# Loading tile 0's x in two halves on two queues, and the parameter transposes one warm-up later

## Chip, cores and metric

The kernel runs on one core of one Trainium2 chip. The metric is the device time of one execution in microseconds (us). The time before is the median of three runs.

## The reference

Two blocks share one layer norm and are added to the residual. Cut to what matters:

```
xn = layernorm(x)                                   # x: 1 x 2048 x 512
A  = 2*Re(sum over states of C * h) + xn*Dskip      # h[t] = Lam_bar*h[t-1] + B_bar*xn[t]
B  = (silu(xn @ w_gate) * (xn @ w_up)) @ w_down     # 512 -> 1376 -> 512
out = x + A + B
```

The state recurrence runs over the 2048 rows with 512 complex states. `Lam_bar` and `B_bar` come from the parameter vectors `log_dt`, `Lambda_re` and `Lambda_im`, of 512 numbers each. Inputs and output are bfloat16.

## The kernel before

The 2048 rows are 16 tiles of 128 rows, in four chunks of four tiles (512 rows). A chunk goes through layer norm, a transposition of the normalised rows (`xnT`), gate and up products, the products with B for the state recurrence, the scan on VectorE, and one accumulated product that joins `w_down` and C. TensorE's instructions and SyncE's are issued in the order in which the program states them (`_CHAIN`). The order on ScalarE, VectorE and GpSimd is chosen by `_schedule`, a list planner with estimated costs: among what could start soonest, within 200 ns, it takes the work with the longest remaining path (plus priorities written by hand). It models the transfers as one pipe that takes them one after the other. `_plan` then gives each DMA a semaphore of its own with a level of 16, and each engine one counting semaphore, and derives the waits.

What the change touches is the start, before TensorE has anything real to do:

- Loads. SP issues, in this order, x of tiles 0, 1 and 2 (128 rows of 1 KB each, `ldx`, all through L438), three slices of `w_gate` by rows of the contraction, x of tile 3, the fourth slice, then larger loads. ACT's queue issues the three parameter loads (`pload`, 4 rows of 256 bytes into `prow`); ScalarE's first activation, with its table load, stands behind the first of them in the trace.
- Statistics of tiles 0, 1 and 3 on VectorE (`ln_stats`: L533 `bn_stats`, L535 `bn_aggr`), then the power -1/2 on GpSimd (L537), and scaling on VectorE (L544) in two parts, columns 0 to 127 and 128 to 511 for tiles 0 and 1. Tile 2's statistics are taken on ScalarE (L552, L554) with GpSimd's L556 and L558, and it is scaled by L567.
- Transposes on TensorE (`xt_part`, L642) of each part, and their evacuation to `xnT`, on VectorE for the first part (L649) and on ScalarE for the others (L654).
- Gate products of the first six column tiles of `w_gate` in quarters (`ffn_gate_quarters`, L835): one matmul of 128 columns for each column tile, row tile and slice of the contraction, ordered by hand so that each uses what has come in by then. From L807 on, products use whole chunks of 512 columns.
- Ahead of all this TensorE runs warm-up matmuls on a constant (`pe_warm`, L508): n of 512 columns and m of 128. Between them stand three small transposes of the parameters (`params_t`, L517), which need the three parameter loads.

TensorE's order at the start is written out thus:

```
pe_warm(7, 0, ta)
params_t(tc)
pe_warm(1, 3, ta)
xt_part(c, 0, 0, ta)
ev00 = xt_part_ev_dve(c, 0, 0, ta)
xt_part(c, 0, 1, tc)
```

Of the kernel before, what the change touches and what calls it, by code (L numbers as in the profile page):

```python
# [31 lines left out]

class _Task:
    __slots__ = ("eng", "fn", "deps", "name", "est", "idx", "dma", "sem", "lvl",
                 "waits", "nsig", "vc", "out", "lat", "bl", "start", "fin", "nbytes", "prio", "ninst", "odeps")

    def __repr__(self):
        return "T(%s,%s)" % (self.eng, self.name)
# [2 lines left out]
class _Graph:  # L41
# [5 lines left out]
    def add(self, eng, fn, reads=(), writes=(), name="", est=100.0, dma=False, after=(), out=False, nbytes=0, prio=0.0, ninst=1, order=()):  # L47
        t = _Task()
        t.eng, t.fn, t.name, t.est, t.dma, t.out, t.nbytes, t.prio = eng, fn, name, float(est), dma, out, nbytes, prio
        t.ninst = ninst  # L50
        t.idx = len(self.tasks)
        deps = set(after)
        for r in reads:
            w = self.last_w.get(r)
            if w is not None:
                deps.add(w)
        for r in writes:
            w = self.last_w.get(r)
            if w is not None:
                deps.add(w)  # L60
            for rd in self.readers.get(r, ()):
                deps.add(rd)
        for r in reads:
            self.readers[r].append(t)
        for r in writes:
            self.last_w[r] = t
            self.readers[r] = []
        deps.discard(t)
        t.deps = deps
        t.odeps = set(o for o in order if o is not None and o not in deps)  # L70
        assert all(o.eng == eng for o in t.odeps)
        t.sem = None
        t.lvl = 0
        t.lat = 0.0
        self.tasks.append(t)
        return t

# [111 lines left out]
def _plan(tasks, streams, new_sem, eng_sems):  # L189
    consumers = defaultdict(list)  # L190
    for t in tasks:
        for d in t.deps:
            consumers[d].append(t)
    for t in tasks:
        if t.dma:
            t.nsig = True
        else:
            t.nsig = any((c.eng != t.eng) or (t.eng != "pe") or c.dma for c in consumers[t])
    last_out = [None, 0]
    for eng, st in streams.items():  # L200
        lvl = 0
        for t in st:
            if t.dma and t.out and not consumers[t]:
                if last_out[0] is None:
                    last_out[0] = new_sem("out_end")
                t.sem = last_out[0]
                last_out[1] += 16
                t.lvl = last_out[1]
            elif t.dma:
                t.sem = new_sem("dma%d" % t.idx)  # L210
                t.lvl = 16
            elif t.nsig:
                lvl += 1
                t.sem = eng_sems[eng]
                t.lvl = lvl
    end_wait = tuple(last_out)
    pos = {e: 0 for e in streams}
    known = {e: {} for e in streams}
    done = set()
    remaining = sum(len(s) for s in streams.values())  # L220
    while remaining:
        progressed = False
        for eng, st in streams.items():
            while pos[eng] < len(st):
                t = st[pos[eng]]
                if any(d not in done for d in t.deps):
                    break
                kn = known[eng]
                waits = {}
                for d in t.deps:  # L230
                    if d.eng == eng and eng == "pe" and not d.dma and not t.dma:
                        continue
                    k = id(d.sem)
                    if kn.get(k, 0) >= d.lvl:
                        continue
                    if k not in waits or waits[k][1] < d.lvl:
                        waits[k] = (d.sem, d.lvl)
                for d in t.deps:
                    for k, v in d.vc.items():
                        if kn.get(k, 0) < v:  # L240
                            kn[k] = v
                t.waits = list(waits.values())
                t.vc = dict(kn)
                if t.sem is not None:
                    t.vc[id(t.sem)] = max(t.vc.get(id(t.sem), 0), t.lvl)
                done.add(t)
                pos[eng] += 1
                remaining -= 1
                progressed = True
        assert progressed, "deadlock in static schedule"  # L250
    outs = [t for t in tasks if t.out]
    held = set()
    todo = [t for t in outs if not consumers[t]]
    while todo:
        t = todo.pop()
        if t not in held:
            held.add(t)
            todo.extend(t.deps)
    assert all(t in held for t in outs)
    return end_wait  # L260
# [11 lines left out]
def bass_parallel_sum__ssm_conv_s5__swiglu_ffn__prompt_kernel(  # L272
# [32 lines left out]
    with es:  # L305
        block = es.enter_context(nc.Block())

        def sb(name, shape, dt):
            return es.enter_context(nc.sbuf_tensor(name, shape, dt))
# [7 lines left out]
        x_sb = sb("x_sb", [128, NT, D], B16)  # L317
# [35 lines left out]
        st = sb("st", [128, NT, 9], F32)  # L353
# [9 lines left out]
        def one_c(n):  # L363
            return nc.const_aps.tensor(1.0, [128, n], B16)
# [57 lines left out]
        def BK(b):  # L422
            return [("bk", b, 0), ("bk", b, 1)]

        x_v = A_x[0].rearrange("(a p) d -> p a d", p=128)
# [5 lines left out]
        def dma(name, dst, src, writes, nbytes, reads=(), after=(), out_=False, eng="sp", xpose=False, prio=0.0, **kw):  # L431
            after = tuple(after)
            if xpose:
                assert eng == "sp"
                fn = lambda e, dst=dst, src=src: e.dma_start_transpose(out=dst, in_=src)
                est, nb = 2000.0, int(nbytes * 1.45)
            else:
                fn = lambda e, dst=dst, src=src: e.dma_start(dst, src, **kw)  # L438
                est, nb = 330.0 + nbytes / 900.0, nbytes
            t = g.add(eng, fn, reads=reads, writes=writes, name=name, dma=True, after=after, out=out_, est=est, nbytes=nb, prio=prio)  # L440
            return t

        TILEB = 128 * D * 2
        FH0 = 6 * 128

        def pload(name, slot, src, **kw):
            dma(name, prow[:, slot, :], src.rearrange("(a p) -> a p", p=128), [("prow", slot)], 1024, **kw)
# [3 lines left out]

        def ldx(a):
            return dma("ld_x%d" % a, x_sb[:, a:a + 1, :], x_v[:, a:a + 1, :], [("x", a)], TILEB)
        pload("ld_ldt", 2, A_log_dt, eng="act")
        pload("ld_lim", 1, A_Lambda_im, eng="act")
        pload("ld_lre", 0, A_Lambda_re, eng="act")
        ldx(0)
        ldx(1)
        ldx(2)
        ldw(0)  # L460
        ldw(1)
# [22 lines left out]
        def loads_wd():  # L484
# [9 lines left out]
              reads=[("ones",)], writes=[("ident",)], name="ident", est=300)  # L494
        g.add("pool", lambda e: e.iota(iot[:], pattern=[[1, TP]], base=0, channel_multiplier=0, allow_small_or_imprecise_dtypes=True),
              writes=[("iot",)], name="iota", est=1000)
# [5 lines left out]
              name="act_warm", est=220, prio=1e6)  # L502

        def pe_warm(n, m, bk):

            def mm(e):
                for w in [512] * n + [128] * m:
                    inst = e.matmul(pbank[:, bk, 0:w], lhsT=one_c(128), rhs=one_c(w), start=True, stop=True)  # L508
                return inst
            g.add("pe", mm, writes=BK(bk), name="pe_warm", est=n * 427 + m * 107, ninst=n + m)  # L510
# [20 lines left out]

        def ln_stats(a, order=()):
            ln_bn[a] = g.add("dve", lambda e, a=a: e.bn_stats(out=st[:, a, 0:6], in_=x_sb[:, a, :]),  # L533
                             reads=[("x", a)], writes=[("st", a)], name="bnst%d" % a, est=640, order=order)
            ln_ag[a] = g.add("dve", lambda e, a=a: e.bn_aggr(out=mv[:, a, :], in_=st[:, a, :]),  # L535
                             reads=[("st", a), ("steps",)], writes=[("mv", a)], name="bnag%d" % a, est=90)
            ln_rs[a] = g.add("pool", lambda e, a=a: e.tensor_tensor(out=rstd[:, a:a + 1], in0=mv[:, a, 1:2], in1=mhalf[:, a:a + 1], op=ALU.pow),  # L537
                  reads=[("mv", a), ("mhalf",)], writes=[("rstd", a)], name="rstd%d" % a, est=600, prio=(3000.0 if a < 4 else 0.0))
# [284 lines left out]
        def ffn_gate_quarters(c, tiles):  # L823
            ta, tb = next_tr(), next_tr()
# [23 lines left out]
                    xt_part_ev(c, a, h, slot)  # L848

            tc = banks[tiles[-1]]  # L850
            pe_warm(7, 0, ta)
            params_t(tc)
            pe_warm(1, 3, ta)
            xt_part(c, 0, 0, ta)
            ev00 = xt_part_ev_dve(c, 0, 0, ta)
            xt_part(c, 0, 1, tc)
# [27 lines left out]
            for i in tiles:  # L884
# [6 lines left out]
                      reads=BK(bk), writes=[("sg", sl)], name="silu%d_%d" % (c, i), est=490)  # L891
# [293 lines left out]
```

## Time and profile before

| what | value |
|---|---|
| median of 3 runs | 178.64 us (178.61 to 178.97) |
| profiled execution | 178.72 us |
| its span, first to last instruction | 177.0 us |
| TensorE matmul busy | 173.4 us (98%) |
| VectorE busy | 162.0 us (92%) |
| ScalarE busy | 101.4 us (57%) |
| GpSimd busy | 15.1 us (9%) |
| moved by DMA | 12.91 MB |

Times in the profile count from the start of the span. A line of the timeline gives start, duration, engine, source line, operation, output and inputs, and in brackets how long the engine was idle before and what ended that. "SPq" and "ACTq" are the issues of transfers on the queues of SyncE and ScalarE; "PEld" is the weight load of TensorE, which overlaps its matmuls. The recorded time of one matmul includes its way through the array; what one costs in a dense row is the distance between starts.

### The profile page before, as it was taken

The page shows a single profiled execution, that of the slowest core. Times are in us where ns is not written, and L with a number is a line of the kernel's source. Part 1 is how long each engine was busy: PE and PEld are TensorE (multiplying, and loading weights), DVE is VectorE, ACT ScalarE, POOL GpSimd, SP SyncE. Part 2 cuts the span into 40 slices and gives each one's busy share as a digit, 9 for nine tenths or more (in the row PEclk, how much of TensorE's full clock was granted, in tenths as well). Part 3 has the DMA queues.
Part 4 walks back from the last instruction along what each step waited for, and adds up shares of the span by engine and source line. Part 5 has one row for each costly group of instructions (what it writes and reads, how often), then busy time and mean ns, then how long its engine had stood idle before and what let it go on. Part 6 is the DMA issues. An engine that isn't in the chain of part 4 may idle for free.

```text
span 177.0 us, 2634 instructions
## 1 busy us (share of the span) xinstructions
PE 173.4 (98%) x948; PEld 86.5 (49%) x956; DVE 162.0 (92%) x342; ACT 101.4 (57%) x201; POOL 15.1 (9%) x38
## 2 busy tenths in 40 slices
PE   8999999999999999999999999999999999999994
PEld 2884644455444444446444444445544444444743
DVE  3687899999989979999999999999999999999983
ACT  4679999999998739896598500620666610000000
POOL 6630500000000280000000000000000000000000
DMA  5999669793000700002008000001110000001012
GB/s 149 267 362 250 118 122 171 181 343 131 0 4 0 148 0 0 0 16 77 32 0 150 0 4 0 0 0 59 59 33 0 2 0 0 0 4 59 30 59 89
DMA packets 25092, 12.91 MB, mean 73 GB/s; under 512 B 17304, under 2 KB 25080, under 8 KB 25080
## 3 DMA queue, kind: packets, MB, share of 16 engines
q1 hardware_dynamic: 25056, 12.75, 28.4%
q8 instruction: 7, 0.11, 0.3%
q14 instruction: 5, 0.04, 0.1%
q10 hardware_dynamic: 24, 0.00, 0.0%
HBM read 6.46 MB, written 2.10 MB: 48 GB/s over the span
## 4 chain that ended last, share of the span: by engine, by line
PE 98%; issue 0%; DVE 0%
PE pb L807 36%; PE pb L1041 21%; PE pb L952 16%; PE pb L1054 16%; PE pb L835 3%; PE pb L917 3%; PE pb L508 2%; PE pb L642 1%; DVE osb L1066 0%; PE pb L517 0%
## 5 line engine op out<-in xcount | busy, mean ns | idle before, releaser
L807 PE MATMUL pb<-xnT,wgu 128*128 128x512 bf16 x296 | 64.7, 379 | 0.0
L807 PEld LDWEIGHTS pb<-xnT,wgu 128*128 128x128 bf16 x296 | 28.9, 98 | 33.7
L994 DVE TENSOR_TENSOR_SCAN vq<-sm,car,vq 128x512 bf16<-128x512 f32 x32 | 39.7, 1274 | 0.1
L1041 PE MATMUL pb<-wd,hT 128*128 128x512 bf16 (+3 forms) x194 | 38.1, 355 | 0.2
L1041 PEld LDWEIGHTS pb<-wd,hT 128*128 128x128 bf16 (+1 forms) x198 | 18.5, 98 | 19.9
L952 PE MATMUL pb<-xnT,BT 128*128 128x512 bf16 x128 | 28.1, 379 | 0.0
L1054 PE MATMUL pb<-W,hss 128*128 128x512 bf16 (+2 forms) x140 | 27.8, 355 | 0.2
L956 ACT ACTIVATE u_sb<-pb 128x512 bf16<-128x512 f32 x32 | 18.6, 594 | 13.2 <-PE pb L952 12.4
L902 ACT ACTIVATE uf<-pb 128x512 bf16<-128x512 f32 x40 | 23.5, 606 | 4.3 <-PE pb L807 2.7
L820 ACT ACTIVATE sg<-pb 128x512 bf16<-128x512 f32 x34 | 20.4, 600 | 2.8 <-PE pb L807 2.6
L1054 PEld LDWEIGHTS pb<-W,hss 128*128 128x128 bf16 x144 | 13.5, 98 | 14.2
L952 PEld LDWEIGHTS pb<-xnT,BT 128*128 128x128 bf16 x128 | 12.5, 98 | 15.1
L904 DVE TENSOR_TENSOR hT<-sg,uf 128x512 bf16<-128x512 bf16 x40 | 16.5, 418 | 2.1 <-ACT uf L902 1.3
L1066 DVE TENSOR_TENSOR osb<-pb,x_sb 128x512 bf16<-128x512 f32 (+2 forms) x18 | 11.2, 627 | 1.7 <-PE pb L1054 1.2
L985 DVE TENSOR_TENSOR scrA<-u_sb,cosT 128x1024 bf16<-128x1024 bf16 x16 | 11.0, 687 | 0.6 <-ACT cosT L772 0.5
L988 DVE TENSOR_TENSOR scrA<-u_sb,sin 128x1024 bf16<-128x1024 bf16 x16 | 11.0, 687 | 0.0
L1004 DVE TENSOR_TENSOR scrA<-vq,sin 128x1024 bf16<-128x1024 bf16 x16 | 11.0, 687 | 0.0
L1000 DVE TENSOR_TENSOR scrA<-vq,cosT 128x1024 bf16<-128x1024 bf16 x16 | 11.0, 685 | 0.0
L990 DVE TENSOR_TENSOR vq<-scrA 128x1024 bf16<-128x1024 bf16 x16 | 10.7, 688 | 0.0
L1009 DVE TENSOR_TENSOR hss<-scrA 128x1024 bf16<-128x1024 bf16 x16 | 10.6, 686 | 0.0
L685 POOL TENSOR_TENSOR sm<-sm 128x4 f32<-128x4 f32 x13 | 5.5, 442 | 39.3 <-ACT sm L706 38.9
L599 ACT ACTIVATE xn_sb<-x_sb,ve,rstd 128x512 bf16<-128x512 bf16 x8 | 6.2, 812 | 2.5 <-DVE ve L597 2.5
(87 smaller groups left out, 132.8 us busy)
## 6 DMA issues: line engine op xcount, KB each, us to landing
out_dram<-osb SPq DMA_DIRECT2D x15, 128.0 KB, 1.7
x_sb<-in_A_x_dram SPq DMA_DIRECT2D x3, 512.0 KB, 4.5
wd<-in_B_w_down_dram SPq DMA_DIRECT2D x1, 1280.0 KB, 8.4
wgu<-in_B_w_gate_dram SPq DMA_DIRECT2D x4, 192.0 KB, 3.5
wgu<-in_B_w_up_dram SPq DMA_DIRECT2D x1, 768.0 KB, 6.8
wgu<-in_B_w_gate_dram SPq DMA_DIRECT2D x1, 608.0 KB, 8.0
wgu<-in_B_w_up_dram SPq DMA_DIRECT2D x1, 608.0 KB, 9.7
x_sb<-in_A_x_dram SPq DMA_DIRECT2D x4, 128.0 KB, 2.1
```

What stands on the lines that cost most here:

```text
L807: inst = e.matmul(pbank[0:fs, bk, :].rearrange("p (j t) -> p j t", j=4), lhsT=w[:, kt, i * 128:i * 128 + fs], rhs=xnT[:, c % 2, :, kt, :], ...
L820: g.add("act", lambda e, sl=sl, bk=bk, fs=fs: e.activation(out=sg[0:fs, sl, :], in_=pbank[0:fs, bk, :], func=AF.Silu), reads=BK(bk), write ...
L902: g.add("act", lambda e, ul=ul, bk=bk, fs=fs: e.activation(out=uf[0:fs, ul, :], in_=pbank[0:fs, bk, :], func=AF.Identity), reads=BK(bk), w ...
L904: g.add("dve", lambda e, sl=sl, ul=ul, fs=fs, i=i, hb=hb: e.tensor_tensor(out=hT[0:fs, hb, i, :], in0=sg[0:fs, sl, :], in1=uf[0:fs, ul, :] ...
L952: inst = e.matmul(pbank[:, bk, :].rearrange("p (j t) -> p j t", j=4), lhsT=BT[:, ri, kt, pt * 128:(pt + 1) * 128], rhs=xnT[:, c % 2, :, kt ...
L956: last_uev[0] = g.add("act", lambda e: e.activation(out=u_sb[:, us, ri, :], in_=pbank[:, bk, :], func=AF.Identity), reads=BK(bk), writes=[ ...
L985: g.add("dve", lambda e, sl=sl, U=U, Cb=Cb: e.tensor_tensor(out=pr2[:, sl, 0], in0=U, in1=Cb, op=ALU.mult), reads=ru + rdt, writes=[("pr", ...
L988: g.add("dve", lambda e, sl=sl, Usw=Usw, S2=S2: e.tensor_tensor(out=pr2[:, sl, 1], in0=Usw, in1=S2, op=ALU.mult), reads=ru + rdt, writes=[ ...
L994: g.add("dve", lambda e, sl=sl, ri=ri, pt=pt, rr=rr, c=c: e.tensor_tensor_scan(out=vq[:, sl, 1, ri, :], data0=rr[:, pt:pt + 1].to_broadcas ...
L1041: inst = e.matmul(pbank[:, bk, 0:nc_], lhsT=hT[0:fs, hb, i, lt * 128:(lt + 1) * 128], rhs=wd[0:fs, i, c0:c0 + nc_], start=(i == 0), stop=F ...
L1054: inst = e.matmul(pbank[:, bk, 0:nc_], lhsT=hss[:, hb, pt, ri, lt * 128:(lt + 1) * 128], rhs=W12[:, ri, pt, c0:c0 + nc_], start=False, sto ...
L1066: g.add("dve", lambda e, bk=bk, a=a, os_=os_, o0=o0, c0=c0, nc_=nc_: e.tensor_tensor(out=osb[:, os_, o0:o0 + nc_], in0=pbank[:, bk, 0:nc_] ...
```

## The change

Tile 0's x becomes two transfers of 64 rows: rows 0 to 63 on SP's queue, in the place of the whole load, and rows 64 to 127 on ACT's queue, stated ahead of the parameter loads. Both raise one semaphore, and whoever waits for tile 0 waits for 32. Only the first statistics of tile 0 name the second half as an input of their own; what follows them is behind that wait. On TensorE the parameter transposes come after eight 512-column warm-up matmuls instead of seven, and three 128-column ones follow; the number of warm-up matmuls is the same.

```diff
@@ _plan: semaphores
+            if t.mate is not None:
+                continue
             if t.dma and t.out and not consumers[t]:
...
+    for t in tasks:
+        if t.mate is not None:
+            t.sem = t.mate.sem
+            t.lvl = t.mate.lvl = 32
@@ loads
+        x0b = dma("ld_x0b", x_sb[64:128, 0, :], x_v[64:128, 0, :], [("x", 0, 1)], TILEB // 2, eng="act")
         pload("ld_ldt", 2, A_log_dt, eng="act")
         pload("ld_lim", 1, A_Lambda_im, eng="act")
         pload("ld_lre", 0, A_Lambda_re, eng="act")
-        ldx(0)
+        x0b.mate = dma("ld_x0", x_sb[0:64, 0, :], x_v[0:64, 0, :], [("x", 0)], TILEB // 2)
@@ ln_stats
-                             reads=[("x", a)], writes=[("st", a)], name="bnst%d" % a, est=640, order=order)
+                             reads=[("x", a)] + ([("x", 0, 1)] if a == 0 else []), writes=[("st", a)], name="bnst%d" % a, est=640, order=order)
@@ ffn_gate_quarters
-            pe_warm(7, 0, ta)
+            pe_warm(8, 0, ta)
             params_t(tc)
-            pe_warm(1, 3, ta)
+            pe_warm(0, 3, ta)
```

More of the change, by code (lines that the diff above doesn't have):

```diff
@@ L34 @@
     __slots__ = ("eng", "fn", "deps", "name", "est", "idx", "dma", "sem", "lvl",
-                 "waits", "nsig", "vc", "out", "lat", "bl", "start", "fin", "nbytes", "prio", "ninst", "odeps")
+                 "waits", "nsig", "vc", "out", "lat", "bl", "start", "fin", "nbytes", "prio", "ninst", "odeps", "mate")
     def __repr__(self):
@@ L74, in add @@
         t.lat = 0.0
+        t.mate = None
         self.tasks.append(t)
```

## The prediction

> **What bounds the kernel now.** I read the page's chain that ended last first, because only a change on that chain can move the end.
>
> ```profile
> PE 98%; issue 0%; DVE 0%
> ```
>
> ```profile
> 0.82 3.15 PE pb L508 x7
> 3.97 0.17 PE pb L517 x3
> 4.14 0.86 PE pb L508 x4
> 5.00 0.23 PE pb L642
> ...
> 7.47 2.35 PE pb L835 x42
> ```
>
> The first line is the share of the span by engine; the others are the chain in order of time (start, us, what). TensorE is the chain from start to end, and after the first 6 us its gaps are 0.05 us pieces marked "issue". So whatever moves the start of its dense work moves the end by as much, provided no later operand is late. L508 are warm-up matmuls on constants and L517 the parameter transposes: fillers. The real work begins at L642, the first transpose of normalised x. The chain credits the fillers up to 5.00 because modelled ends of matmuls overlap; whether the fillers or x set that start, I read from the timeline of the first 6 us (start, us, engine, line, tile, idle time before it and its releaser).
>
> ```profile
> 2.89 0.69 DVE L533 BATCH_NORM_STATS2 st<-x_sb 128x6 f32<-128x512 bf16 x1 [2.89 <-DMA x_sb<-in_A_x_dram]
> 3.69 0.20 DVE L535 BATCH_NORM_AGGREGATE mv<-st 128x2 f32<-128x9 f32 x1
> 3.97 0.56 POOL L537 TENSOR_TENSOR rstd<-mv,mhalf 128x1 f32<-128x1 f32 x1 [0.80 <-DVE mv L535]
> 4.60 0.57 DVE L544 TENSOR_SCALAR xn_sb<-x_sb,mv,rstd 128x128 bf16<-128x128 bf16 x2
> 4.94 0.10 PEld L642 LDWEIGHTS pb<-ident,xn_sb 128*128 128x128 bf16 x1 [0.20 <-DVE xn_sb L544]
> ```
>
> This is a serial chain: x of tile 0 lands, statistics (DVE), power (GpSimd), scaling (DVE), first transpose (TensorE). The weight load for that transpose starts 0.05 us after the 128-column scaling ended (4.60 + 0.28 = 4.88), with 0.20 idle before it, released by the scaling. So x is the limit here. But only just: in the trace the last 128-column warm-up matmul starts at 4.68, and such matmuls stand 0.107 us apart, so the fillers were done at 4.79 and the transpose began at 4.94. TensorE lost about 0.15 us.
>
> Then the transfers, in slices of 0.1 us (columns: start:end, length, busy time of PE, PEld, DVE, ACT, POOL, clock, DMA share, GB/s) and the issues on ACT's queue.
>
> ```profile
> 1.80:1.90 0.10, 0.10 (x2) 0.00 (x0) 0.00 (x0) 0.10 (x1) 0.10 (x1) 1.00 0.33 102
> 1.90:2.00 0.10, 0.10 (x1) 0.00 (x0) 0.00 (x0) 0.10 (x1) 0.10 (x1) 1.00 0.48 146
> 2.00:2.10 0.10, 0.10 (x2) 0.04 (x1) 0.00 (x0) 0.10 (x1) 0.10 (x1) 1.00 0.42 154
> 2.20:2.30 0.10, 0.10 (x2) 0.01 (x1) 0.00 (x0) 0.10 (x1) 0.10 (x2) 1.00 1.06 379
> ```
>
> ```profile
> 0.79 0.56 ACTq L438 DMA_DIRECT2D prow<-in_A_log_dt_dram  x1
> 1.38 1.28 ACT L501 ACT_TABLE_LOAD   x1 [1.38 <-PEq L1170]
> 1.45 0.26 ACTq L438 DMA_DIRECT2D prow<-in_A_Lambda_im_dram  x1
> 1.74 0.31 ACTq L438 DMA_DIRECT2D prow<-in_A_Lambda_re_dram  x1
> ```
>
> Tile 0's load is issued at 0.79, its first bytes move at 1.8, and for 0.3 us the 16 DMA engines are less than half busy; from 2.2 they are full. Its semaphore reaches its count at 2.86.
>
> **The change, part by part.** *Halves.* Removed: one 128-row load on SP. Added: 64 rows on SP and 64 on ACT. Both spread over the same engines, so the bytes per engine stay. What can shrink is the half-empty start. From the slices, 10 + 15 + 15 + 28 + 38 KB had moved by 2.30 and the remaining 25 of the 131 KB by 2.37. At 379 GB/s from 1.80 on, all would have moved by 2.15, so the bound on the good side is 0.22 us earlier. On the bad side only ACT's three loads of 4 rows speak, which touched 4 engines each: the first took 0.56 us to issue (SP's first load took 0.40), and its four packets went out at 1.73, 1.74, 1.98 and 2.10. If a load over 16 engines spread four times as far (1.5 us), its last engine would start near 3.2 and, with 0.25 us for four rows and the 0.34 us that tile 0's load needed from last packet to landing, land at 3.8, 0.95 later. Between these I take the row that is nearest in kind, tile 0's load itself on SP, whose engines started within about 0.2 us of each other: half of the lost 0.22 comes back, x lands 0.11 us earlier.
>
> The Trainium skill speaks against this: "DMA: Bandwidth & Descriptors", section "Rules for kernel authors", says of two transfers to disjoint partition halves not to bother, since both halves use the same 16 engines. By it the term is 0; the half-empty slices are what makes me weigh more than 0.
>
> *What the path makes of 0.11.* Statistics, power, scaling and transpose follow each other, so each moves with the landing. The stops are, in order: the fillers; the second tile's statistics, which ran at 3.81 behind tile 0's although x of tile 1 was there at 3.34 (0.4 spare); the first weight slice, landed at 5.33 and used at 5.60 (0.25 spare); tile 2's scaling, done at 6.85 from its own load and ScalarE's statistics, whose transposes load at 7.03 (0.13 spare with the 0.05 handover); tile 3's scaling, done at 9.40 for 9.60 (0.15 spare). After tile 2 the matmuls are dense, so up to 0.13 travels to the end undiminished.
>
> *Fillers.* The order is now eight 512-column matmuls, three parameter transposes, three of 128 columns: the same eleven matmuls and transposes. The seventh 512 started at 3.33, spaced 0.427: the eighth ends at 4.19, the transposes start 0.14 after that (as 3.90 after 3.76), 0.17 later the small ones (as 4.07 after 3.90), three by 0.107: free at 4.82. The first transpose of x can move from 4.94 to 4.82 at best, a cap of 0.12, just above the 0.11.
>
> *Parameters, one matmul later.* All three parameter loads now stand behind the half on ACT's queue, as does the table load. Issuing the half costs between 0.26 (ACT's second load) and 0.70 (ACT's first, 0.56, plus the 0.14 that SP's 0.43 is above the 0.29 of ACT's later ones). The last parameter load, issued at 1.74 and landed at 3.54, moves to between 2.0 and 2.45 and lands at 3.8 to 4.25. Its consumer, the transposes on TensorE, now start at 4.33 instead of 3.90: covered, with 0.05 to 0.5 to spare. Without this cover each 0.1 us would delay the three small warm-ups and the first transpose queued behind it, once beyond the 0.11 still left to x. The table load (1.28 us, then a 0.20 activation, done at 2.88) shifts by the same 0.26 to 0.70, to 3.6 at worst; ScalarE's next work waits for tile 2's x at 3.83. Covered. The parameters' evacuation follows a ScalarE copy at 5.76: nothing.
>
> *SP's queue.* Tile 1's load and those behind it follow a half instead of a whole. The issue may shrink from 0.40 towards 0.26, or not at all: 0 to 0.14 earlier, feeding only the spare times above. Value 0.
>
> *One wait for both halves.* DVE waits once, for the doubled count; behind it stand all its other operations, and GpSimd and TensorE wait on those. It costs nothing beyond the later half.
>
> Sum: -0.11 us. The profiled execution took 178.72 (span 177.0 and 1.7 around it) and would take 178.61; against the median, 178.64, that is 178.53.
>
> **Rivals.**
>
> *No gain.* The engines or a shared generation of descriptors limit the load, two queues bring it in at the same 2.86, and nothing moves: 178.64. For it: DMA share 1.06 at 2.2, so there is no room in the second half of the transfer. Against: shares of 0.33 to 0.48 before.
>
> *ACT's half is late.* The wait for the whole load is replaced by one for a half that is slower than the whole. For it: ACT's first issue took 0.16 us longer than SP's, with 4 rows. An issue of 0.70 ends 0.30 after SP's did; less the 0.11 for fewer rows, x lands 0.2 later. It decides from the moment when ACT's half lands after 2.86, and then every 0.1 is 0.1 at the end: 178.84, or up to 179.6 with the 0.95 above. Against: ACT's first packets went out at 1.73, before SP's 1.82.
>
> *The clock.* Matmuls of 128 columns stand 0.107 apart until 5.84 and 0.056 after, though the clock column says 1.00 throughout. If a changed pattern of fillers postponed this by the 3 us that 54 matmuls take there, they would take 5.8: near 181. Against: the fillers are the same eleven, within 0.05 us of the same end. The Trainium skill, "TensorE: Matmul & The Clock Gate", Part 1, has a free-running activity window of about 3.4 us for this, and by that rule a small change of the fillers would rarely matter.
>
> *Another order.* The planner sees x land at the same modelled time, since it adds the two halves one after the other; the following loads shift by a few ns. A flipped choice between equals could give some tenths of a us either way.
>
> **How the numbers follow.** Chances: forecast 0.52, no gain 0.22, late half 0.19, clock 0.02, order 0.05. A difference under 0.2% (0.36 us) is about what a measurement of this kernel can't tell from no change; its three runs span 178.61 to 178.97. The first two cases and the milder half of the third stay inside it. Slower by more: 0.08 from the late half, 0.02 clock, 0.03 order and spread: 0.13. Faster by more: order and spread, 0.05, since the fillers cap the mechanism at 0.12. Range: from the full cap less a spread of 0.1 (178.40) to the late half at 0.3 (178.95); outside lie the worse half of the late case, the clock and flipped orders, and some spread.
>
> **What would show it.** Right: the first statistics (L533) start near 2.78; the first L642 weight load at 4.83 to 4.85 with little idle before it; L517 near 4.33, not waiting for its loads; L835 dense as before and the 42 matmuls at 7.36 instead of 7.47. No gain: L533 still at 2.89. Late half: L533 after 2.89, the L642 idle above 0.20, everything behind shifted by the same amount. Wrong altogether: L517 after 4.4, or the spacing of L835 at 0.107 beyond 6 us, or a gap before tile 2's or tile 3's transposes.

## The result: 180.56 us, slower, and the profile after

The changed kernel takes 180.56 us (median of 4 runs, 180.44 to 180.86) against 178.70 before (178.61 to 178.97): a ratio of 1.0104, 95% interval 1.0089 to 1.0119. Forecast was 178.53, a little faster, in a range up to 178.95. Its profiled execution took 180.44 us with a span of 178.7.

The page's chain by engine, and the chain in order of time (start, us, what). The change adds eight lines to the source, so before's L508, L517, L533, L642, L807, L835 are now L516, L525, L541, L650, L815, L843.

```profile
PE 96%; DMA 1%; DVE 1%; issue 0%
```

```profile
0.80 2.57 DMA x_sb<-in_A_x_dram
3.39 0.70 DVE st L541
...
5.37 0.29 PE pb L650
...
7.22 1.39 PE pb L843 x13
8.61 0.43 PE pb L650 x4
9.04 2.54 PE pb L843 x42
...
13.81 8.63 PE pb L815 x40
```

The same two places in the chain before:

```profile
6.42 0.83 PE pb L835 x13
...
12.05 8.63 PE pb L807 x40
```

The chain no longer runs through the fillers: it begins with the load of x. L815, at 12.05 before (as L807), starts at 13.81. All of the loss, 1.76 us in these two traces, is there; from then on the two chains are alike. And the loss has two parts. At the first transpose (L650, 5.37 against 4.94) it is 0.43. The other 1.33 comes between 5.4 and 13.8: thirteen matmuls take 1.39, where before 13 took 0.83.

The timeline shows what is late:

```profile
3.39 0.69 DVE L541 BATCH_NORM_STATS2 st<-x_sb 128x6 f32<-128x512 bf16 x1 [3.39 <-DMA x_sb<-in_A_x_dram]
4.65 0.21 PE L525 MATMUL pb<-ident,prow 4*128 4x4 bf16 x3 [0.25 <-DMA prow<-in_A_Lambda_re_dram]
5.36 0.10 PEld L650 LDWEIGHTS pb<-ident,xn_sb 128*128 128x128 bf16 x1 [0.33 <-DVE xn_sb L552]
```

Statistics wait for x until 3.39 (2.89 before). The parameter transposes, which had waited for nothing, now wait for the last parameter row: in the trace it lands at 4.56 (3.54 before), and the eighth warm-up matmul was through at 4.19. Then the first transpose waits for x. So TensorE stands still twice ahead of its real work, for 0.46 us (4.19 to 4.65) and for 0.27 (5.09, when the last filler was through, to 5.37). The brackets on TensorE's own lines say less, since they count from the end of the last recorded matmul.

Where the transfers lost the time, from the issues and the slices of 0.1 us:

```profile
0.79 0.57 SPq L445 DMA_DIRECT2D x_sb<-in_A_x_dram  x1
0.80 0.55 ACTq L445 DMA_DIRECT2D x_sb<-in_A_x_dram  x1
1.46 0.67 ACTq L445 DMA_DIRECT2D prow<-in_A_log_dt_dram  x1
```

```profile
2.00:2.10 0.10, 0.10 (x2) 0.04 (x1) 0.00 (x0) 0.10 (x1) 0.10 (x1) 1.00 0.00 0
2.10:2.20 0.10, 0.10 (x2) 0.10 (x1) 0.00 (x0) 0.10 (x1) 0.10 (x2) 1.00 0.17 41
2.20:2.30 0.10, 0.10 (x2) 0.01 (x1) 0.00 (x0) 0.10 (x1) 0.10 (x1) 1.00 0.41 102
```

Each half takes 0.55 to 0.57 us to issue, longer than the whole had (0.40), on SP as well as on ACT. The first bytes move at 2.15, not at 1.82, and the parameter load behind ACT's half takes 0.67 where such a load had taken 0.26 to 0.56.

And the matmul rate, for the gate products alone: the profile after (L843), then the one before (L835). The number in brackets is the count of matmuls.

```profile
7.40:8.40 1.00, 1.00 (x12) 0.94 (x9) 1.00 0.88 301
9.40:10.40 1.00, 1.00 (x21) 1.00 (x19) 1.00 1.01 283
```

```profile
7.40:8.40 1.00, 1.00 (x20) 1.00 (x20) 1.00 1.01 281
```

TensorE is "busy" all the time in both, and the clock column says 1.00, yet there are 12 matmuls in the stretch after and 20 before. In the trace the distance between starts falls from 0.107 to 0.056 us at 5.87 before, and at 9.32 after: 3.45 us later. The recorded length of one matmul of 128 columns shows it as well: 0.31 us before that step, 0.22 behind it. The first stretch lies wholly before that step in the kernel after, the second wholly behind it.

### The profile page after: what moved, and what is told of

It reads as the page before. It is cut to its first block, busy times and chain, and to the rows that moved or that the text cites. A ratio compares the mean times of both kernels' runs of the same rounds, so it can differ in the third digit from the quotient of the medians.

```text
span 178.7 us, 2643 instructions
## 1 busy us (share of the span) xinstructions
PE 175.2 (98%) x956; PEld 87.9 (49%) x956; DVE 162.0 (91%) x342; ACT 101.4 (57%) x201; POOL 14.9 (8%) x38
## 4 chain that ended last, share of the span: by engine, by line
PE 96%; DMA 1%; DVE 1%; issue 0%
PE pb L815 36%; PE pb L1049 21%; PE pb L1062 15%; PE pb L960 15%; PE pb L843 4%; PE pb L925 3%; DMA x_sb<-in_A_x_dram 1%; PE pb L650 1%; DVE st L541 1%; DVE mv L543 0%; DVE osb L1074 0%; DVE xn_sb L552 0%
## 5 line engine op out<-in xcount | busy, mean ns | idle before, releaser
L815 PE MATMUL pb<-xnT,wgu 128*128 128x512 bf16 x296 | 64.7, 379 | 0.0
L815 PEld LDWEIGHTS pb<-xnT,wgu 128*128 128x128 bf16 x296 | 28.9, 98 | 33.7
L1049 PE MATMUL pb<-wd,hT 128*128 128x512 bf16 (+3 forms) x198 | 38.8, 355 | 0.0
L1062 PE MATMUL pb<-W,hss 128*128 128x512 bf16 (+2 forms) x144 | 28.3, 355 | 0.0
L541 DVE BATCH_NORM_STATS2 st<-x_sb 128x6 f32<-128x512 bf16 x7 | 4.5, 680 | 3.5 <-DMA x_sb<-in_A_x_dram 3.4
```

The source lines that it names most:

```text
L815: inst = e.matmul(pbank[0:fs, bk, :].rearrange("p (j t) -> p j t", j=4), lhsT=w[:, kt, i * 128:i * 128 + fs], rhs=xnT[:, c % 2, :, kt, :], ...
L1049: inst = e.matmul(pbank[:, bk, 0:nc_], lhsT=hT[0:fs, hb, i, lt * 128:(lt + 1) * 128], rhs=wd[0:fs, i, c0:c0 + nc_], start=(i == 0), stop=F ...
L1062: inst = e.matmul(pbank[:, bk, 0:nc_], lhsT=hss[:, hb, pt, ri, lt * 128:(lt + 1) * 128], rhs=W12[:, ri, pt, c0:c0 + nc_], start=False, sto ...
```

## Experiments

Theory 1: two causes. x is late and costs about 0.43 to 0.6 itself; and TensorE's idle time ahead of its real work postpones the faster clock, which costs the rest. Rival, theory 2: late x alone does all of it. A third blames the moved transposes. Edits are given against the kernel named.

**halves_only** (against the changed kernel)

```diff
-            pe_warm(8, 0, ta)
+            pe_warm(7, 0, ta)
             params_t(tc)
-            pe_warm(0, 3, ta)
+            pe_warm(1, 3, ta)
```

> Tile 0 in two halves on two queues as in the changed kernel, TensorE's order as before (seven 512-column warm-ups, parameter transposes, one 512 and three 128). Theory 1 (two causes: x lands 0.5 us late, and TensorE's wait for the late parameters postpones the faster clock): the parameter transposes wait from 3.76 to about 4.6, the matmul spacing of 0.107 us lasts to about 9.3 us, and the fillers behind the transposes end near 5.6, a little after x is ready: 180.4 to 180.7 us. Theory 2 (x late alone postpones the clock): 180.4 to 180.6, the same. A theory in which the moved transposes are to blame: 178.7 to 179.2.

180.84 us (180.61 to 181.05), ratio 1.0113 (1.0097 to 1.0130). The transposes of the parameters ran at 4.59, and the spacing changed at 9.48. The load alone makes the loss. The median lies 0.28 above that of the changed kernel and 0.14 above what theory 1 had let expect, but the runs of the two kernels overlap (180.61 to 181.05 and 180.44 to 180.86), so it is not shown that moving the transposes saved anything.

**params_only** (against the kernel before: the other half of the change)

```diff
-            pe_warm(7, 0, ta)
+            pe_warm(8, 0, ta)
             params_t(tc)
-            pe_warm(1, 3, ta)
+            pe_warm(0, 3, ta)
```

> Tile 0 in one load as before, only TensorE's order changed (eight 512-column warm-ups, parameter transposes, three of 128). Theories 1 and 2: the parameters are there at 3.54 and x at 2.86, no new wait, first transpose of x at 4.94, spacing 0.056 from 5.9 on: 178.6 to 178.8 us. A theory in which the moved transposes are to blame: over 179.5.

178.71 us, ratio 0.9999 (0.9991 to 1.0008). With whole loads the moved transposes are free. The third theory is out.

**after_fill9** (against the changed kernel)

```diff
-            pe_warm(8, 0, ta)
+            pe_warm(9, 0, ta)
```

> The changed kernel with a ninth 512-column warm-up ahead of the parameter transposes, which covers the wait for the parameters (4.19 to 4.65); x still lands 0.5 us late. Theory 1 (the wait at the parameter transposes postpones the clock): spacing 0.056 from about 5.9 on, what is left is the late x, 0.43 us: 179.0 to 179.3 us. Theory 2 (the late x postpones the clock): spacing 0.107 to about 9.3 as in the changed kernel: 180.4 to 180.6.

179.31 us (179.20 to 179.48), ratio 1.0028 (1.0017 to 1.0039): more work on TensorE, and 1.25 us faster than the changed kernel. Chain of this kernel:

```profile
6.42 0.22 PE pb L843 x4
6.65 0.18 PE pb L650 x3
6.83 0.82 PE pb L843 x13
```

Thirteen matmuls take 0.82 again, though x was as late (statistics at 3.28, first transpose at 5.40). So of the 1.86 us some 0.6 are late x and 1.25 late clock. The trace of this one execution does not show the wait covered: the step came at the ninth warm-up matmul (0.38 us at 4.19, where the one at 3.76 took 0.59), and TensorE then still stood waiting for the parameters, which landed at 4.79. What carries the reading is that none of the six runs was late.

**before_warm6** and **before_warm5** (against the kernel before): idle time with nothing late

```diff
-            pe_warm(7, 0, ta)
+            pe_warm(6, 0, ta)      # before_warm5: 5
```

> The kernel before with six 512-column warm-ups ahead of the parameter transposes instead of seven; x and parameters land as before. TensorE idles 0.3 us ahead of the parameter transposes (3.33 to 3.6) and about 0.5 ahead of the first transpose of x. Theory 1 (idle time of TensorE alone postpones the clock, whatever made it): spacing 0.107 to about 9.3, and 1.3 us more than before: 179.9 to 180.2 us. Theory 2 (it takes late x): 178.6 to 178.8.

> The kernel before with five 512-column warm-ups instead of seven; x and parameters in time, TensorE idles about 0.7 us ahead of the parameter transposes and 0.45 ahead of the first transpose of x. Theory 1: the postponed clock in more of the runs than with six warm-ups (4 of 10 there), most at 180.0 to 180.3 us, the others at 178.6 to 179.0. Theory 2: 178.6 to 179.0 in all.

With six, 178.85 us as the median of two groups: six runs at 178.61 to 179.00 and four at 179.99 to 180.21 (the trace is of one of the six). With five, all four runs lie at 180.29 to 180.61 (ratio 1.0097, 1.0082 to 1.0112), above the 180.0 to 180.3 that was expected of most. With seven, none of the 76 runs of the kernel before is above 179.18. Timeline of the kernel with five:

```profile
3.65 0.21 PE L517 MATMUL pb<-ident,prow 4*128 4x4 bf16 x3 [0.54 <-DMA prow<-in_A_Lambda_re_dram]
3.80 0.93 PE L508 MATMUL pb<-const-bfloat16-1.0 128*128 128x512 bf16 x4
5.01 0.79 PE L642 MATMUL pb<-ident,xn_sb 128*128 128x128 bf16 x4 [0.29 <-DVE xn_sb L544]
```

x and parameters come as before to within 0.1, and the first transpose starts at 5.01; what is gone are two dummy matmuls, 0.85 us of filling. The loss of 1.7 us is the clock's: here the spacing changes at 9.73.

**x0_second** and **x0_second_fill** (against the kernel before)

```diff
-        ldx(0)
-        ldx(1)
+        ldx(1)
+        ldx(0)
@@ x0_second_fill, also:
-            pe_warm(1, 3, ta)
+            pe_warm(2, 3, ta)
```

> The kernel before, whole loads, but SP issues tile 1's x ahead of tile 0's, so x of tile 0 lands where tile 1's did (3.34), as late as in the changed kernel, while the parameters come in time and no two large issues collide. Theory 1 (the late x costs its own 0.43 us; the clock is postponed where TensorE idles too much in a row of some 3.4 us, and what matters is the sum of idle time): idle is about 0.6 us ahead of the first transpose of x instead of 0.27 there and 0.46 at the parameters, less than in the changed kernel: 179.1 to 179.3 us, in some runs 180.3 to 180.6. Theory 2 (late x alone postpones the clock): 180.4 to 180.6 in all.

> The kernel with tile 0's x as SP's second load (x 0.43 us late, four of five runs at 180.35 to 180.9) with one more 512-column warm-up behind the parameter transposes, which fills TensorE's wait for x (4.79 to 5.35). Theory 1 (idle time of TensorE postpones the faster clock): 179.15 to 179.35 us in all runs. Theory 2 (late x itself does): unchanged, 180.4.

Without the filler 180.43 us, one run at 179.35 and four at 180.35 to 180.90; with it 179.20 (179.06 to 179.27 in ten runs), ratio 1.0025 (1.0015 to 1.0035). x is late in both. The run without the filler alone spoke for theory 2: four of five runs lie near the 180.4 to 180.6 that it named for all, where theory 1 had let expect that for some only. The run with it decides: late x is worth 0.5; the rest needs the idle time. Theory 2 has fallen.

Next, why x lands late. Theory A: two issues over 16 engines at once slow each other. Theory B: ACT's queue is slow for large loads.

**halves_on_sp** (against the kernel before; the first statistics wait for both halves, as in the change)

```diff
-        ldx(0)
+        dma("ld_x0", x_sb[0:64, 0, :], x_v[0:64, 0, :], [("x", 0)], TILEB // 2)
+        dma("ld_x0b", x_sb[64:128, 0, :], x_v[64:128, 0, :], [("x", 0, 1)], TILEB // 2)
```

> The kernel before with tile 0's x in two loads of 64 rows, both on SP's queue, one after the other; parameters as before. Theory A (an issue over 16 engines costs about 0.41 us whatever its rows, and slows when ACT issues one at the same time): each half takes about 0.40 us to issue, the second lands near 3.2, x is 0.3 to 0.4 us late, every load behind it by 0.45: 179.0 to 179.2 us, in some runs 180.3 to 180.5. Theory B (ACT's queue is slow for large loads, SP's halves are cheap): issues of 0.25, x at 2.9, 178.7.

```profile
0.79 0.56 SPq L438 DMA_DIRECT2D x_sb<-in_A_x_dram  x1
...
1.41 0.58 SPq L438 DMA_DIRECT2D x_sb<-in_A_x_dram  x1
```

179.48 us (179.37 to 179.70), ratio 1.0042 (1.0027 to 1.0056). Both theories are wrong: with nothing large on ACT each half still takes 0.56 to 0.58. x lands at 3.62. This kernel also bears on the clock, since TensorE waits long for x and yet no run is late:

```profile
5.62 0.57 PE L643 MATMUL pb<-ident,xn_sb 128*128 128x128 bf16 x3 [0.62 <-DVE xn_sb L545]
```

**x0_on_act** (against the kernel before)

```diff
+        dma("ld_x0", x_sb[:, 0:1, :], x_v[:, 0:1, :], [("x", 0)], TILEB, eng="act")
         pload("ld_ldt", 2, A_log_dt, eng="act")
...
-        ldx(0)
```

> The kernel before with tile 0's whole x on ACT's queue ahead of the parameters, while SP begins with tile 1's x. Theory A: two issues over 16 engines at once, both take about 0.55 us instead of 0.40 and both tiles land near 3.3 to 3.5. Theory B (ACT's queue is slow): SP's issue stays at 0.40 and tile 1 lands at 2.86, tile 0 at 3.3 or later. In both the parameters come late, near 4.5, so 180.4 to 181 us by theory 1 of the clock.

Two whole loads issued at the same moment take 0.41 (ACT) and 0.40 us (SP). Neither A nor B. They do share what follows: SP's tile lands at 3.37, where SP's first load landed at 2.86 before; tile 0's statistics start at 3.58, the last parameter row lands at 5.25, and the kernel takes 180.83 us (two runs).

**act_16rows** (against the changed kernel)

```diff
-        x0b = dma("ld_x0b", x_sb[64:128, 0, :], x_v[64:128, 0, :], [("x", 0, 1)], TILEB // 2, eng="act")
+        x0b = dma("ld_x0b", x_sb[112:128, 0, :], x_v[112:128, 0, :], [("x", 0, 1)], TILEB // 8, eng="act")
...
-        x0b.mate = dma("ld_x0", x_sb[0:64, 0, :], x_v[0:64, 0, :], [("x", 0)], TILEB // 2)
+        x0b.mate = dma("ld_x0", x_sb[0:112, 0, :], x_v[0:112, 0, :], [("x", 0)], TILEB * 7 // 8)
```

> The changed kernel with 112 rows of tile 0 on SP and only 16 on ACT, one for each of the 16 engines. Theory A, with a cost per engine: both issues still take about 0.55 us and x lands at 3.2 to 3.4. Theory A with a cost per row, or theory B: SP's issue 0.40, x at 2.8 to 3.0, and the time is 178.8 to 179.0, unless the parameters are late enough to postpone the clock.

Issues of 0.40 and 0.42, x at 3.01, 178.84 us, ratio 1.0003 (0.9992 to 1.0014): the loss is gone, with two queues and one semaphore as in the change. That left the number of rows.

**rows_ladder** (against the kernel before; `ldxs` makes two loads of one tile, cut at the row named, and the statistics wait for both)

```diff
         ldx(0)
-        ldx(1)
-        ldx(2)
+        ldxs(1, 0, 96, 128)      # 96 + 32 rows, two loads
+        ldxs(2, 0, 80, 128)      # 80 + 48
...
-        ldx(3)
+        ldxs(3, 0, 64, 128)      # 64 + 64
```

> The kernel before, with SP's loads of tiles 1, 2 and 3 cut into 96 + 32, 80 + 48 and 64 + 64 rows; tile 0 whole. One look at the time that each issue takes (so far: 128 rows 0.40 to 0.43 us, 112 rows 0.40, 16 rows 0.42, 64 rows 0.55 to 0.58). Theory C (64 rows alone are slow): 96, 32, 80 and 48 take 0.40 to 0.43 and the two of 64 take 0.55 to 0.58. Theory D (every load of fewer than 112 and more than 16 rows is slow): all six take 0.55 or so. Theory E (only the first issues of a program with an uncommon shape are slow): the first of each new size 0.55, the second 64 at 0.43. The time itself says little: later loads are late, 178.9 to 181 us.

SP's issues of 96, 32, 80, 48 and twice 64 rows, each from its own stretch of the timeline:

```profile
1.24 0.41 SPq L438 DMA_DIRECT2D x_sb<-in_A_x_dram  x1
1.71 0.41 SPq L438 DMA_DIRECT2D x_sb<-in_A_x_dram  x1
2.17 0.44 SPq L438 DMA_DIRECT2D x_sb<-in_A_x_dram  x1
2.65 0.42 SPq L438 DMA_DIRECT2D x_sb<-in_A_x_dram  x1
4.53 0.55 SPq L438 DMA_DIRECT2D x_sb<-in_A_x_dram  x1
5.13 0.59 SPq L438 DMA_DIRECT2D x_sb<-in_A_x_dram  x1
```

Theory C: 64 rows, and of these sizes only 64, are slow, the second time as the first. Time of this one run: 179.08 us.

**rows_80_48** (against the changed kernel): only the row counts moved off 64

```diff
-        x0b = dma("ld_x0b", x_sb[64:128, 0, :], x_v[64:128, 0, :], [("x", 0, 1)], TILEB // 2, eng="act")
+        x0b = dma("ld_x0b", x_sb[80:128, 0, :], x_v[80:128, 0, :], [("x", 0, 1)], TILEB * 3 // 8, eng="act")
...
-        x0b.mate = dma("ld_x0", x_sb[0:64, 0, :], x_v[0:64, 0, :], [("x", 0)], TILEB // 2)
+        x0b.mate = dma("ld_x0", x_sb[0:80, 0, :], x_v[0:80, 0, :], [("x", 0)], TILEB * 5 // 8)
```

> The changed kernel with tile 0 cut into 80 rows on SP and 48 on ACT, both counts without a slow issue in the ladder, the rest of the change as it is. If the count of 64 rows is the whole reason for the late x: issues of 0.40 to 0.44 us, first bytes at 1.82, x lands between 2.9 and 3.1, the last parameter row near 4.1 to 4.2, no wait at the parameter transposes, spacing 0.056 by 6.6 at the latest: 178.7 to 179.0 us. If two queues with large parts slow each other as well: issues over 0.5, x at 3.2 or later, 179.2 to 180.6. If halves bring the forecast gain once their size is right: x at 2.75, 178.6.

```profile
0.79 0.42 ACTq L445 DMA_DIRECT2D x_sb<-in_A_x_dram  x1
0.79 0.40 SPq L445 DMA_DIRECT2D x_sb<-in_A_x_dram  x1
```

```profile
4.33 0.23 PE L525 MATMUL pb<-ident,prow 4*128 4x4 bf16 x3
```

178.80 us, ratio 1.0008 (0.9999 to 1.0017). x lands at 2.96, the last parameter row at 4.08, and the transposes at 4.33 wait for nothing. The count of 64 rows was the cause of the slow issue, and the whole loss hangs on it: what is left, 0.08 us, this measurement can't tell from nothing.

**cols_halves** (against the changed kernel): each queue takes 128 rows, half the columns

```diff
-        x0b = dma("ld_x0b", x_sb[64:128, 0, :], x_v[64:128, 0, :], ...
+        x0b = dma("ld_x0b", x_sb[:, 0, 256:512], x_v[:, 0, 256:512], ...
-        x0b.mate = dma("ld_x0", x_sb[0:64, 0, :], x_v[0:64, 0, :], ...
+        x0b.mate = dma("ld_x0", x_sb[:, 0, 0:256], x_v[:, 0, 0:256], ...
```

> The changed kernel, but tile 0 is cut by columns: all 128 rows of 512 bytes on each of the two queues. Theory C or D (the count of rows makes the issue slow): both issues 0.40 to 0.42, first bytes at 1.82, x lands between 2.75 and 3.05, the last parameters near 4.2 in time for TensorE at 4.33: 178.6 to 178.95 us. If two large issues at once are slow whatever their rows: issues of 0.55, x near 3.35, 179.2 to 180.6.

Issues of 0.41 and 0.40; x at 3.07; 179.00 us, ratio 1.0010 (1.0001 to 1.0020), both just above what was expected. Each load moves as many bytes as a half of 64 rows, so it isn't the bytes that make the issue slow. And a split that issues as fast as a whole load still doesn't bring x in earlier.

## Why the prediction was wrong, step by step

**What bounds the kernel** held. TensorE is the chain, the start of its dense work sets the end, and what was lost before L815 is the whole loss.

**Halves, -0.11: the step that failed first, in sign and size.** x landed 0.50 later. I took the cost of issuing a half to lie between two rows, a load of 4 rows and one of 128, and so never above 0.40 on SP. It was 0.57: of the sizes tried, 64 alone is out of line. The row that I trusted most, SP's own whole load, was thus no guide to a half, on SP as little as on ACT. Without that the term would still not have been a gain: at 80 + 48, 112 + 16 and by columns x landed at 2.96, 3.01 and 3.07, where SP's first whole load lands at 2.86 to 2.96 in the traces of the kernels with nothing of x on ACT. The half-empty slices at the start were not filled from the second queue: at 80 + 48 SP's first packet goes out at 1.82 and ACT's only at 1.98. The Trainium skill, "DMA: Bandwidth & Descriptors", "Rules for kernel authors", which says not to bother with two transfers to disjoint partition halves, was right here: no split gained (178.80, 178.84, 179.00).

**Parameters, "covered with 0.05 to 0.5 to spare": failed.** The half's issue, 0.55, was inside my 0.26 to 0.70. I added only that to the last parameter load; the load behind the half took 0.67 instead of 0.56, and the last one was issued at 2.44, just inside my 2.0 to 2.45. What went past them was its way from issue to landing, which I had carried over as it stood: 2.12 us instead of 1.80. It took 1.93 to 2.12 in all six kernels with a part of tile 0 ahead of it on ACT's queue, against 1.72 to 1.91 in the seven with tile 0 whole and nothing of x on ACT. So the last row landed at 4.56, not by 4.25. The table load, which I had moving with the half, stayed at 1.38, which cost nothing. The price named for lost cover, 0.1 for 0.1, was also wrong: it left out what idle time does to the clock.

**The clock, a rival with 0.02: this was the larger part**, 1.25 of 1.86 us. I had its mechanism and its row, but argued that "the fillers are the same eleven, within 0.05 us of the same end". That hung on the parameters coming in time. I also took from the window that a small change of the fillers would rarely matter; here two waits of 0.46 and 0.27 us mattered in four runs of four. Late x and late parameters leave TensorE idle, and that idle time is what postponed the clock. Its price, 2.8 us, was too high: it took 54 matmuls, while in the profile after some 30 real ones lie between 6.2 and the step at 9.32, and 30 x 0.051 = 1.5, of which waits hide a part.

**Late half, 0.19**: right in direction and in "every 0.1 is 0.1 at the end" for x itself (0.43 at the transpose for 0.50 of landing; in halves_on_sp, where no run is late by the clock, 0.72 at the end for 0.75); its nominal 0.2 should have been 0.5, and it was both halves.

**Fillers**: their order and spacing were as worked out: in params_only and rows_80_48 the transposes start at 4.33, as forecast. **Another order** didn't happen: VectorE and GpSimd run the same operations in the same order as before. **SP's queue**: a half frees it later, not earlier (tile 1's load issued at 1.42 instead of 1.25).

**What stays open.** Why 64 rows are slow to issue: not tried. And the exact rule of the step. By the times of the runs, it moved in all of the changed kernel, halves_only, x0_on_act and before_warm5, in some of before_warm6 and x0_second, and in none of halves_on_sp, where TensorE waited 0.83 us ahead of the first transpose of x (4.79 to 5.62), longer than the 0.57 in x0_second. In the one trace of halves_on_sp that transpose already has the short record (0.23 us), so there the step came during the wait. The Trainium skill, "TensorE: Matmul & The Clock Gate", Part 1, describes a free-running window of 3.4 us; the step of 3.45 us and the two groups of runs agree with that. In the traces that were on time the step lies anywhere from before 4.2 (cols_halves) to 6.4 (rows_ladder), in the late ones from 9.1 to 10.0. How much idle time in a window is too much these runs don't say, only that in a given place more of it postpones more often (0, 4 of 10, 4 of 4).

## What to carry to other kernels

Dummy matmuls ahead of the real work are not only a start-up cost: a wait put between them, here 0.46 us for a 1 KB load, can keep TensorE at half rate until 9.3 us instead of 5.9. So what a filler waits for belongs early in its queue, and a spare filler at a wait is insurance: it brought back 1.25 us in after_fill9 and 1.23 in x0_second_fill (what it costs where nothing is late was not measured). When a load is moved ahead of others in a queue, cost the issue and the landing of each that stands behind it, not the moved one alone. And price a transfer of a new shape from that shape; between two neighbouring sizes a third can be slower than both.

## What the runs showed of the hardware that was not expected

- A load of 64 rows of 1 KB took 0.54 to 0.59 us to issue on SP and on ACT; 16, 32, 48, 80, 96, 112 and 128 rows took 0.39 to 0.44. The issue behind it is slow too: a whole load took 0.56 to 0.58 behind a half, in halves_only 0.82, where it takes 0.41 otherwise. From issue to first byte a half that was first on its queue needed 1.33 to 1.61 us, SP's first whole load 1.02 to 1.04.
- Two whole loads issued together on two queues don't slow each other's issue (0.41 and 0.40), but they delay landings: SP's landed at 3.37, where it lands at 2.86 to 2.96 with none on ACT beside it.
- TensorE at half rate shows in no busy share and not in the clock column (1.00 throughout), only in the distance between starts (0.107 against 0.056 us for 128 columns), the count of matmuls in a stretch and the recorded length of one (0.31 against 0.22 us).
